# Batch 5's q by way of DRAM and DMA transposes, and every step in a new order

## The chip, the cores and the metric

The kernel runs on one core of one Trainium2 chip. A core has five engines that each take instructions in their own order: TensorE (PE in the profile; its weight loads stand apart as PEld), VectorE (DVE), ScalarE (ACT), GpSimd (POOL) and SyncE (SP). DMAs are issued by two of them: SP issues DMAs on a hardware queue, GpSimd on a software queue. The metric is the device time of one execution in microseconds.

## The reference

Two parts follow each other. Sliding-window causal attention over 8 batches of 8 heads, 576 positions and 64 channels; then a two-layer network on the result, laid out as 4608 tokens of 512 channels.

```python
scores = scale * np.matmul(q, k.transpose(0, 1, 3, 2))
rel = pos[:, None] - pos[None, :]
mask = (rel >= 0) & (rel < 64)
attn = softmax(np.where(mask, scores, -1e9))
x = np.matmul(attn, v).transpose(0, 2, 1, 3).reshape(4608, 512)
h = x @ w_in                       # 512 x 2048
g = h - np.tanh(h)
out = g @ w_out                    # 2048 x 512
```

(The softmax is written out in the reference; it is abbreviated here.) Inputs and output are float32; the kernel works in bfloat16 with float32 sums.

## The kernel before, in words

Heads are taken in pairs: pair g = 4b + r holds heads r and r + 4 of batch b, so there are 32 pairs. Tokens of x are taken in nine chunks of 512, and the 2048 hidden channels in sixteen parts m of 128. Each of these small pieces of work is a *step*, a Python function that issues its instructions; `STEPS` (line 557) gives every step a short name, and `PLAN` (line 581) is one long string of such names. `play` reads it from left to right, so **the order of the words is the order of the instructions on every engine and on every queue**; the scheduler is switched off (`tc.manual_schedule()`), and semaphores make a step wait for its inputs and for its buffers. A letter at the end of a name selects the engine: p GpSimd, a ScalarE, v VectorE, s SP. The steps that matter here:

- `lk`, `lq` (line 92) load k or q of a pair, `LQ.b` (line 114) loads q of a whole batch (576 KB), `lv`, `lt`, `LV.b.i` load v, `lr` (line 173) loads rows of k, `wi.0` to `wi.2` (line 189) load w_in in three parts and `wo.0` to `wo.3` w_out. All but the very first are issued on GpSimd's queue and cast to bfloat16 on the way.
- q reaches the layout of the scores in one of two ways. *By TensorE* (batches 0 to 5 before): `cq` (lines 88 or 90) rearranges the pair's rows into `qb`, `Ep.g` (line 261) makes six 96-row transposes into PSUM, and two evictions `Ea.g` and `Eb.g` (lines 88 or 90) write the halves of `qT`. *By DMA* (batches 6 and 7 before): `cz.g` (two copies on GpSimd, line 128) spreads the rows into `qz[g % 2]`, whose other columns are zero; `bo.g` (SP, line 133) writes that to DRAM, and `td.g` (SP, line 138) reads it back with a transposing DMA into `qT[g % 2]`. `z` (line 235) clears both `qz` once, on GpSimd; `mk` (line 220) clears pads of `kw`.
- k is transposed on TensorE (`Fp`, `Fc`) for batches 0 to 2, and by `tk.b.i` (SP, line 181), a transposing DMA from the loaded rows into `kw[b % 2]`, for batches 3 to 7.
- `Rp.g.i` are the scores of a third of a pair (three matmuls, line 300), `Rx` the exponentials (ScalarE, line 305), `M` the masking (VectorE, line 393). `Z.b` (VectorE, lines 166 and 167) copies v's rows across partition halves, in two copies, for the windows that straddle two blocks; `PP.g` (36 matmuls, line 418) multiplies two pairs by v and needs `Z`. `DR` and `DN` normalise.
- x is transposed on TensorE for batches 1 and 2 (`Xp`, `Xc`) and by SP's transposing DMAs (`Y.b`, line 472) from batch 3 on.
- `H.c.m` (four matmuls, line 487), `A.c.m` (tanh on ScalarE, line 495), `G.c.m` (subtraction on VectorE, line 501), `W.c.s.p` (four matmuls, line 526) and `O.c.s` (eviction and output DMA, line 542) are the network. `U.n` are n matmuls on zeros that fill TensorE's early waits.

`qT`, `qz`, `kw`, `vw` and the loaded rows of q and k exist twice, taken in turn, so a load waits until the last reader of two batches (or two pairs) earlier is done. In the steady part the words of attention for batch b + 2 or so stand among those of the network on earlier chunks.

The way by DMA in code:

```python
def cast_q(g):
    i = stage.pop((g, "q")).rearrange("p h (e d) -> p h e d", d=D)
    for h in range(2):
        nc.gpsimd.tensor_copy(qz[g % 2][:, h, :, 64 * h:64 * h + 64], i[:, h])

def bounce(g):
    t = dram.tile([2, S, 128], BF16, tag="q", name="qd")
    nc.sync.dma_start(out=t.rearrange("h (p e) c -> p h (e c)", e=E),
                      in_=qz[g % 2].rearrange("p h e c -> p h (e c)"))
    rows[g, "qd"] = t

def tr_dma(g):
    nc.sync.dma_start(out=qT[g % NR].rearrange("c h s -> c (h s)"),
                      in_=rows.pop((g, "qd")).rearrange("h s c -> (h s) c"), transpose=True)
```

Of the kernel before, what the change touches and what calls it, by code (L numbers as in the profile page):

```python
# [15 lines left out]
def kernel(  # L16
# [21 lines left out]
    M = d_ff // 128  # L38
# [515 lines left out]
    def subtract(c, m, s=None):  # L554
# [4 lines left out]
        z=lambda: [more_zeros(i) for i in range(2)],  # L559
# [16 lines left out]
    def play(script):  # L576
# [5 lines left out]
        mt.0 mv.0 mt.1 lk.3.p lq.0.s lk.1.p u ck.1.a lq.1.p LV.0.1 cq.0.a lk.0.s i mv.1 U.11 cq.1.v mq.1 U.1  # L582
        LV.0.3 Ep.1.3 Fp.1.2 Ec.1.3.v lq.3.p ck.0.v U.4 U.1.3 h Fc.1.2.a LV.0.2 Fp.0.2 LV.0.0 LV.0.4 Rp.1.1.4
        lk.2.p Ep.0.3 Ec.0.3.v lq.2.p Fc.0.2.a Rx.1.1.4 Rp.1.0.0 Rp.0.1.4 Rx.1.0.0 Fp.3.2 Ep.3.3 Rx.0.1.4
        Rp.0.0.0 Fc.3.2.v Z.0 Ec.3.3.a Rx.0.0.0 U.4 lk.5.p lk.7.p lq.5.p lk.6.p n Rp.3.1.4 P.0 Fp.2.2 D.0 Ep.2.3
        Rp.3.0.0 Fc.2.2.a lq.4.p lk.4.p Ec.2.3.v lq.7.p U.2 ck.5.v Rx.3.0.0 P.1 Rx.3.1.4 Fp.5.3 cq.5.v Rp.2.0.0
        Fc.5.3.a Rp.2.1.4 Rx.2.0.0 D.1 Rx.2.1.4 Ep.5.3 Xp.0.0.1.2 lv.1.1.1 P.3 wi.0 Eb.5.3.v wi.1 ck.4.v
        Ea.5.3.a wi.2 Xc.0.0.1.2.a Fp.4.3 Fc.4.3.a Rp.5.0.4 lv.1.1.0 lq.6.p D.3 lt.1 cq.4.v P.2 Rx.5.0.4
        lv.1.0.1 lv.1.0.0 Xp.0.0.0.3 Rp.5.1.4 D.2 Xc.0.0.0.3.a U.1.2 Xp.0.1.0.3 Xp.0.1.1.2 Rx.5.1.4 Xc.0.1.1.2.v
        U.1 mq.0 Rp.5.2.4 Xc.0.1.0.3.a H.0.1 A.0.1 H.0.0 ck.7.v Rx.5.2.4 G.0.1 H.0.2 wo.0 za.1.1.p lq.8.p A.0.0  # L590
        G.0.0 A.0.2 Ep.4.3 H.0.4 Eb.4.3.a wo.1 Ea.4.3.a A.0.4 ck.6.v G.0.2 H.0.3 Fp.7.3 Rp.4.2.4 lk.8.p H.0.5
        A.0.3 N Fc.7.3.v zb.1.0.p Rx.4.2.4 G.0.3 Fp.6.3 A.0.5 zb.1.1.p Rp.4.0.4 Rx.4.0.4 G.0.5 H.0.6 Rp.4.1.4
        G.0.4 A.0.6 Fc.6.3.a G.0.6 wo.2 wo.3 H.0.8 cq.6.v lq.9.p H.0.7 lk.9.p cq.7.v H.0.9 A.0.8 G.0.8 A.0.7
# [36 lines left out]
        G.3.2 tk.5.0 Ep.20.3 H.3.3 cq.22.a Rp.18.2.4 lr.6.1.1 lr.6.4.0 Rx.18.2.4 LV.5.2 H.3.4 lr.7.2.1 cq.23.v  # L630
# [75 lines left out]
```

## Time and profile before

| | |
|---|---|
| runs | 314.80, 314.82, 316.29 us; median 314.82 |
| the profiled execution | 316.02 us, its span 314.2 us |
| TensorE matmuls busy | 302.0 us, 96% of the span |
| VectorE, ScalarE, GpSimd busy | 188.3, 171.2, 111.4 us |
| first matmul of the network (H.0.1) | 25.58 us |
| last matmul ends | 310.7 us |
| DMA packets of the software queue | 69.1% of 16 engines' span |
| qd<-qz writes on SP | 8, 288 KB each, 3.4 us to landing |

The page gives busy time of each engine over the whole span; the windows cut it by stage, the list of waits tells for what an engine stood still, and the timeline shows single instructions in order of their start. A matmul record has the time from its start to its modelled end, so neighbouring matmuls overlap in the timeline; the time that a step takes from TensorE is the distance between the starts of neighbouring groups. A few matmul records are missing, so a gap of one matmul (0.216 us) inside a group of H or W is not a pause.

### The profile page before, as it was taken

The numbers are of one execution on the slowest core, as the hardware profiler recorded it, in microseconds if no ns is written. First come the engines' busy times: TensorE is split into PE (matmuls) and PEld (weight loads), VectorE is DVE, ScalarE is ACT, GpSimd is POOL, SyncE is SP. The second block draws the span as 40 slices with busy tenths as digits, with TensorE's granted clock in tenths as the row PEclk, the third lists the DMA queues.
The fourth block names the chain that finished last, engine by engine and source line by source line (L and its number), as shares of the span: only waits on it lengthen the run. The fifth ranks groups of instructions, "written<-read, shape, count | busy, mean of one in ns | idle before, by whom it ended". The sixth has DMA issues, their size and how long they took to land.

```text
span 314.2 us, 6083 instructions
## 1 busy us (share of the span) xinstructions
PE 302.0 (96%) x2385; PEld 165.1 (53%) x2413; DVE 188.3 (60%) x323; ACT 171.2 (55%) x320; POOL 111.4 (35%) x164
## 2 busy tenths in 40 slices
PE   6988999998999999999999999999999999999995
PEld 2565555655655556555555545555554444544444
DVE  1685987699857876667655545864674434343400
ACT  3677865488956867657355536444333543433311
POOL 8990655769909460492532540000000000000000
PEclk9999999999999999999999999999999999999999
DMA  9999999999999999997999996581004110010111
GB/s 156 149 169 206 170 203 147 184 102 153 131 147 119 143 184 165 132 133 160 166 167 193 195 202 154 111 179 40 34 35 109 57 45 33 33 37 33 67 69 67
DMA packets 113133, 39.11 MB, mean 124 GB/s; under 512 B 96336, under 2 KB 107600, under 8 KB 113104
## 3 DMA queue, kind: packets, MB, share of 16 engines
q0 software_dynamic: 72064, 18.06, 69.1%
q1 hardware_dynamic: 41040, 20.65, 28.9%
q8 instruction: 19, 0.31, 0.4%
q14 instruction: 10, 0.08, 0.1%
HBM read 36.70 MB, written 11.80 MB: 154 GB/s over the span
## 4 chain that ended last, share of the span: by engine, by line
PE 82%; POOL 6%; DMA 5%; DVE 4%; issue 1%; ACT 1%; POOLq 0%; DVEq 0%; ACTq 0%
PE ps L526 38%; PE ps L487 34%; DMA qall<-in_q_dram 5%; PE ps L300 4%; PE ps L418 3%; DVE gT L501 2%; POOL kall L108 1%; POOL vw L160 1%; PE ps L261 1%; POOL qall L108 1%; PE ps L519 1%; POOL wi L189 1%; PE ps L453 1%; DVE vw L167 1%; DVE qb L90 1%
## 5 line engine op out<-in xcount | busy, mean ns | idle before, releaser
L501 DVE TENSOR_TENSOR gT<-ps,th 128x512 bf16<-128x512 f32 x144 | 97.3, 688 | 80.6 <-ACT th L495 80.0
L487 PE MATMUL ps<-xT,wi 128*128 128x512 bf16 x576 | 141.6, 379 | 0.5 <-DMA wi<-in_moe_w_in_dram 0.3
L526 PE MATMUL ps<-w_out_sb,gT 128*128 128x512 bf16 x532 | 131.8, 379 | 1.4
L495 ACT ACTIVATE th<-ps 128x512 f32<-128x512 f32 x144 | 84.7, 597 | 78.3 <-PE ps L487 74.9
L487 PEld LDWEIGHTS <-wi 128*128 128x128 bf16 x576 | 62.0, 113 | 49.7 <-DMA wi<-in_moe_w_in_dram 0.5
L526 PEld LDWEIGHTS <-gT 128*128 128x128 bf16 x560 | 53.1, 98 | 56.9
L305 ACT ACTIVATE pt<-ps 128x384 bf16<-128x384 f32 (+2 forms) x92 | 45.8, 503 | 20.7 <-PE ps L300 19.5
L176 POOL DMA_DIRECT2D kall<-in_k_dram x50 | 37.1, 758 | 26.5 <-DMA kw<-kall 16.2
L160 POOL DMA_DIRECT2D vw<-in_v_dram x35 | 30.5, 877 | 11.2 <-PE ps L418 8.3
L88 ACT ACTIVATE ysb<-ps 128x512 f32<-128x512 f32 (+1 forms) x23 | 13.3, 578 | 28.4 <-PE ps L526 25.9
L393 DVE TENSOR_TENSOR pt<-pt,ps 128x1152 bf16<-128x1152 bf16 x28 | 20.7, 747 | 2.3 <-ACT pt L305 2.2
L300 PEld LDWEIGHTS <-kw 128*128 128x128 bf16 x180 | 14.4, 98 | 11.7 <-issue 0.4
L88 ACT ACTIVATE qt<-ps 64x576 bf16<-64x576 bf16 x30 | 19.3, 642 | 1.3 <-PE ps L300 0.3
L300 PE MATMUL ps<-qt,kw 128*128 128x128 bf16 x180 | 19.0, 219 | 0.0
L128 POOL COPY qz<-qall 96x384 bf16<-96x384 bf16 x16 | 7.6, 521 | 22.6 <-DMA qd<-qz 12.0
L438 DVE TENSOR_TENSOR xs<-ps,rcp 128x384 bf16<-128x384 f32 x28 | 15.0, 549 | 0.1
L418 PE MATMUL ps<-vw,pt 128*64 128x65 bf16 x504 | 10.7, 197 | 1.5 <-DVE vw L167 1.5
L418 PEld LDWEIGHTS <-pt 128*64 128x64 bf16 x504 | 9.3, 111 | 4.5 <-issue 2.8
L90 DVE COPY ysb<-ps 128x512 f32<-128x512 f32 x14 | 9.6, 686 | 2.6 <-PE ps L526 2.6
L225 PE MATMUL ps<-warm 128*128 128x512 bf16 x26 | 8.9, 478 | 2.2 <-DVE warm L206 2.1
L261 PE MATMUL ps<-ident,qb 96*128 96x96 bf16 x132 | 9.3, 206 | 1.4 <-DVE qb L90 1.4
L261 PEld LDWEIGHTS <-qb 96*128 96x128 bf16 x132 | 7.5, 97 | 4.5 <-DVE qb L90 1.9
(69 smaller groups left out, 169.6 us busy)
## 6 DMA issues: line engine op xcount, KB each, us to landing
out_dram<-ysb SPq DMA_DIRECT2D x35, 256.0 KB, 2.2
vw<-in_v_dram POOLq DMA_DIRECT2D x28, 128.0 KB, 6.0
qall<-in_q_dram POOLq DMA_DIRECT2D x5, 576.0 KB, 8.2
kall<-in_k_dram POOLq DMA_DIRECT2D x40, 64.0 KB, 5.6
qd<-qz SPq DMA_DIRECT2D x8, 288.0 KB, 3.4
w_out_sb<-in_moe_w_out_dram POOLq DMA_DIRECT2D x4, 512.0 KB, 9.2
kall<-in_k_dram POOLq DMA_DIRECT2D x11, 144.0 KB, 5.0
qall<-in_q_dram POOLq DMA_DIRECT2D x11, 144.0 KB, 5.0
```

Source lines behind the costliest of these rows:

```text
L88: nc.scalar.activation(o, i, ACT.Copy)
L160: nc.gpsimd.dma_start(out=w[:, 2 * i + 1, :, 0:D] if i < NF else w[64:128, 2 * i, :, 0:D], in_=v[b, :, 128 * i:128 * i + n].rearrange("h p ...
L176: nc.gpsimd.dma_start(out=token_rows(b)[0:c, i, :, h, :], in_=k[b, NP * h:NP * h + NP, 128 * i:128 * i + c].rearrange("r p d -> p r d"))
L261: nc.tensor.transpose(tp[:, e, :], src[:, e, :], ident[:P, :P])
L300: nc.tensor.matmul(sp[:, i], kt[:, 64 * j:64 * j + 128], qT[g % NR][:, :, 64 * j:64 * j + 64], start=first, stop=first or i == n - 1)
L305: nc.scalar.activation(PT[g % NPT][:, js[0]:js[0] + len(js), :].rearrange("p i (h t) -> p i h t", h=2), sp, ACT.Exp, scale=scale)
L393: nc.vector.tensor_tensor(p, p, mask.unsqueeze(1).to_broadcast([128, 2 * NJ, 64]), ALU.mult)
L418: nc.tensor.matmul(ps[r, bank, 65 * i:65 * i + 65], PT[(g + r2) % NPT][:, j, r], vw[b % 2][:, j, p0 + r2 + NP * h, :], start=True, stop=True)
L487: nc.tensor.matmul(hp, w_in_tile(ki, m), chunk_tile(c)[:, n.start // 64:n.stop // 64, ki % 2, 64 * (ki // 2):64 * (ki // 2) + 64], start=( ...
L495: nc.scalar.activation(th[:, n], hp, ACT.Tanh)
L501: nc.vector.tensor_tensor(gT[c][:, m, columns(s)], hp, th, ALU.subtract)
L526: nc.tensor.matmul(yp, gT[c][:, m, s * 128:(s + 1) * 128], w_out_sb[:, m, :], start=n == 1 and i == 0, stop=n == 4 and i == 3)
```

## The change

Batch 5's q (pairs 20 to 23) is taken out of the way by TensorE and put on the way by DMA: `cq.20` to `cq.23`, `Ep.20` to `Ep.23` and `Ea`, `Eb` of these pairs go; `cz.20` to `cz.23`, `bo.20` to `bo.23` and `td.20` to `td.23` come. No function is changed or added, and the number of all other steps is the same; but the whole `PLAN` is written in a new order, and about thirty evictions and casts (the letter at the end) go from ScalarE to VectorE or the other way. Among the moved steps: the order of the loads ahead of `wi.0`, `wi.1` and `wi.2`; `z`, which stood between `Ea.10` and `G.1.0` and now stands after `Eb.6`; `Y.3`, `tk.5` and `LQ.5` to `LQ.7`; and one `U.1.2`, which stood after `Ep.13`.

On SP's queue, the order from `O.1.2` to `O.2.2` was

```
O.1.2 Y.3 O.1.3 tk.5.4 tk.5.1 tk.5.2 O.2.0 tk.5.0 tk.5.3 O.2.1 bo.25 O.2.2
```

and is

```
O.1.2 Y.3 bo.20 O.1.3 tk.5.0 O.2.0 tk.5.1 tk.5.3 bo.21 td.20 bo.22 tk.5.2 tk.5.4 td.21 O.2.1 bo.23 O.2.2
```

Of the diff, the lines of PLAN that hold the steps spoken of:

```diff
--- before.py
+++ after.py
@@ -579,100 +579,100 @@
...
     PLAN = """
...
-        Fc.5.3.a Rp.2.1.4 Rx.2.0.0 D.1 Rx.2.1.4 Ep.5.3 Xp.0.0.1.2 lv.1.1.1 P.3 wi.0 Eb.5.3.v wi.1 ck.4.v
-        Ea.5.3.a wi.2 Xc.0.0.1.2.a Fp.4.3 Fc.4.3.a Rp.5.0.4 lv.1.1.0 lq.6.p D.3 lt.1 cq.4.v P.2 Rx.5.0.4
-        lv.1.0.1 lv.1.0.0 Xp.0.0.0.3 Rp.5.1.4 D.2 Xc.0.0.0.3.a U.1.2 Xp.0.1.0.3 Xp.0.1.1.2 Rx.5.1.4 Xc.0.1.1.2.v
...
-        G.0.4 A.0.6 Fc.6.3.a G.0.6 wo.2 wo.3 H.0.8 cq.6.v lq.9.p H.0.7 lk.9.p cq.7.v H.0.9 A.0.8 G.0.8 A.0.7
...
-        Rx.8.1.4 Rp.9.0.4 H.1.1 A.1.0 Eb.10.3.v A.1.1 H.1.2 cq.11.v Ea.10.3.v Fp.10.3 z G.1.0 Rx.9.0.4 G.1.1
...
-        Ea.11.3.a Eb.11.3.a G.1.5 mk H.1.7 lr.4.0.1 A.1.6 Rp.10.0.4 H.1.8 Ep.12.3 tk.3.2 LV.3.2 A.1.7 Z.2
...
-        U.1.2 Rp.11.2.4 lr.4.2.1 H.1.13 DN.8.2 Eb.13.3.a G.1.11 tk.3.1 Rx.11.2.4 DN.8.0 tk.3.0 H.1.14 LV.3.1
...
-        A.2.2 Eb.15.3.a G.2.2 Rp.14.1.4 LV.3.4 H.2.5 O.1.1.v Rx.14.1.4 Rp.14.0.4 Rx.14.0.4 H.2.4 A.2.5 Z.3
...
-        G.2.8 LV.4.3 G.2.9 lr.5.0.0 LQ.5 Rp.17.0.4 LV.4.2 Rx.17.0.4 PP.14 Eb.16.3.a DR.14 W.1.3.0 H.2.10
...
-        Rx.17.2.4 Rp.16.1.4 A.2.13 G.2.12 H.2.14 M.17 lr.5.3.1 Y.3 lr.5.1.1 cq.21.a A.2.14 LV.5.0 O.1.3.v
-        Rx.16.1.4 G.2.13 W.2.0.0 Ea.18.3.v tk.5.4 H.2.15 Eb.18.3.a cq.19.v A.2.15 tk.5.1 G.2.14 W.2.0.1 Ep.19.3
-        Rp.18.1.4 Rx.18.1.4 lr.5.3.0 LV.5.4 Ea.19.3.a Eb.19.3.a W.2.0.2 M.16 tk.5.2 H.3.0 G.2.15 A.3.0 cq.20.v
...
-        G.3.2 tk.5.0 Ep.20.3 H.3.3 cq.22.a Rp.18.2.4 lr.6.1.1 lr.6.4.0 Rx.18.2.4 LV.5.2 H.3.4 lr.7.2.1 cq.23.v
-        W.2.1.0 W.2.1.1 tk.5.3 DR.16 Ea.20.3.a M.18 LV.5.1 LQ.6 A.3.3 G.3.3 H.3.5 W.2.1.2 A.3.4 Eb.20.3.a
-        lr.6.2.1 Rp.19.2.4 lr.7.0.1 A.3.5 Ep.21.3 Rx.19.2.4 G.3.4 H.3.6 Rp.19.0.4 G.3.5 cz.25 DN.16.1 A.3.6
-        Rx.19.0.4 H.3.7 W.2.1.3 Rp.20.0.4 DN.16.0 lr.7.1.0 A.3.7 Rx.20.0.4 G.3.6 G.3.7 H.3.8 O.2.1.v Eb.21.3.a
-        Rp.20.2.4 A.3.8 DN.16.2 lr.6.3.0 H.3.9 lr.6.4.1 W.2.2.0 Rx.20.2.4 A.3.9 M.19 Ea.21.3.a PP.18 G.3.9 bo.25
-        G.3.8 Rp.21.1.4 H.3.11 Rx.21.1.4 Rp.20.1.4 H.3.10 Ep.22.3 DR.18 W.2.2.1 Eb.22.3.v W.2.2.2 A.3.10 LV.5.3
...
-        tk.6.2 Ea.22.3.a Rp.21.2.4 Ep.23.3 bo.24 A.3.13 M.20 G.3.10 H.3.12 G.3.13 W.2.3.1 W.2.3.2 DN.18.2 A.3.12
-        Rx.21.2.4 DN.18.0 G.3.12 Eb.23.3.a Ea.23.3.a Rp.22.1.4 H.3.14 cz.27 Y.4 Rx.22.1.4 H.3.15 Z.5 M.21 A.3.14
-        Rp.23.1.4 tk.6.4 G.3.14 bo.27 W.2.3.3 A.3.15 Rx.23.1.4 G.3.15 O.2.3.v PP.20 DR.20 H.4.1 cz.26 LV.6.4
...
-        lr.7.1.1 W.3.1.1 lr.7.3.0 LQ.7 LV.6.3 H.4.8 A.4.7 A.4.8 G.4.7 W.3.1.2 G.4.8 H.4.9 td.24 DR.22 A.4.9
...
-        A.5.2 G.5.2 H.5.4 W.4.0.3 A.5.3 td.27 G.5.3 M.25 tk.7.1 H.5.5 LV.7.0 Rp.27.1.4 cz.30 Rp.27.2.3 A.5.4
...
+        Rp.0.0.0 LV.0.4 Rx.0.0.0 ck.5.a lq.2.p mk Fc.3.2.v lk.2.p U.2 Z.0 Rp.3.1.4 P.0 U.1.3 Ep.2.3 lq.5.p
...
+        Rp.2.1.4 D.1 n lv.1.0.0 U.1.2 lv.1.0.1 Ep.5.3 Rp.2.0.0 Rx.2.1.4 lq.7.p lq.4.p Ea.5.3.v P.3 wi.0 U.1.2
+        D.3 Rx.2.0.0 lq.6.p Xp.0.0.1.2 cq.4.v wi.1 Eb.5.3.a Fp.4.3 Fc.4.3.a P.2 Xp.0.0.0.3 Xc.0.0.0.3.a D.2
+        lk.7.p Rp.5.0.4 N Xc.0.0.1.2.v Rx.5.0.4 Xp.0.1.0.3 Xc.0.1.0.3.v Xp.0.1.1.2 Rp.5.1.4 wi.2 Ep.4.3
...
+        H.0.6 A.0.6 Rp.4.1.4 H.0.7 wo.1 Fc.6.3.a lq.9.p G.0.5 za.1.1.p zb.1.1.p A.0.7 wo.2 H.0.8 Ep.7.3 A.0.8
...
+        Rp.7.0.4 PP.4 cq.8.v Eb.6.3.a z H.0.14 lk.10.p lq.11.p lq.10.p G.0.12 H.0.13 lk.11.p zb.1.3.p A.0.14
...
+        A.1.7 Z.2 G.1.6 Rx.11.1.4 PP.8 tk.3.2 Rp.11.0.4 G.1.7 H.1.9 lr.5.4.1 A.1.8 H.1.10 G.1.8 Rx.11.0.4
...
+        Rp.12.0.4 Xp.2.1.0.3 lr.4.4.0 Rx.12.0.4 G.1.14 W.1.0.3 Xc.2.1.0.3.v Rp.13.2.4 Ep.14.3 O.1.0.a H.2.1 LQ.5
+        Eb.14.3.v Rx.13.2.4 A.2.1 G.2.1 Rp.13.1.4 H.2.0 W.1.1.0 LV.3.4 Ea.14.3.a W.1.1.1 lr.4.4.1 Rx.13.1.4
...
+        H.2.5 Z.3 O.1.1.v PP.12 tk.4.0 A.2.5 Rx.14.0.4 cz.21 G.2.2 tk.4.4 H.2.4 DR.12 lr.5.2.1 Rp.15.2.4
...
+        H.2.6 cz.20 Rx.14.2.4 Ea.17.3.a H.2.9 M.15 A.2.6 Rp.17.1.4 lr.5.0.0 A.2.9 Ep.16.3 M.14 O.1.2.a G.2.6
...
+        G.2.10 H.2.12 G.2.11 A.2.12 lr.6.4.0 H.2.13 Y.3 cq.19.v G.2.12 W.1.3.3 Rx.16.2.4 lr.5.1.1 A.2.13
+        Rp.17.2.4 bo.20 Ep.18.3 H.2.14 Rx.17.2.4 O.1.3.a Rp.16.1.4 A.2.14 G.2.13 lr.5.2.0 Ea.18.3.a Rx.16.1.4
+        M.17 LV.4.2 lr.5.3.1 lr.5.1.0 G.2.14 H.2.15 A.2.15 M.16 lr.5.3.0 G.2.15 W.2.0.0 H.3.0 W.2.0.1 H.3.1
+        Eb.18.3.v tk.5.0 Rp.18.1.4 A.3.0 A.3.1 Ep.19.3 G.3.0 Rx.18.1.4 lr.5.4.0 W.2.0.2 Rp.18.0.4 H.3.2
...
+        H.3.3 LV.5.0 tk.5.1 tk.5.3 PP.16 Rp.18.2.4 W.2.1.0 bo.21 td.20 cz.22 Rx.18.2.4 M.18 Rp.19.2.4 bo.22
+        A.3.3 Rx.19.2.4 H.3.4 A.3.4 Rp.19.0.4 G.3.3 W.2.1.1 H.3.5 W.2.1.2 DR.16 G.3.4 lr.7.3.0 tk.5.2 tk.5.4
+        DN.16.1 H.3.6 W.2.1.3 A.3.5 G.3.5 H.3.7 DN.16.0 Rx.19.0.4 A.3.6 DN.16.2 lr.6.4.1 td.21 cz.23 O.2.1.a
+        Rp.20.0.4 cz.24 A.3.7 G.3.6 M.19 lr.6.3.1 H.3.8 G.3.7 W.2.2.0 PP.18 W.2.2.1 DR.18 Rx.20.0.4 A.3.8 G.3.8
...
+        Rp.20.1.4 G.3.9 Rx.20.1.4 lr.6.0.1 bo.23 H.3.11 Rp.21.0.4 Rx.21.0.4 O.2.2.v H.3.10 Rp.21.2.4 DN.18.2
+        A.3.11 A.3.10 M.20 LV.5.2 G.3.11 td.22 Rx.21.2.4 W.2.3.0 cz.25 W.2.3.1 DN.18.0 H.3.13 G.3.10 td.23
...
+        lr.6.2.0 Rx.25.0.3 tk.6.2 H.4.8 bo.27 LV.6.0 td.24 A.4.8 G.4.7 Rp.25.1.4 LV.7.1 H.4.9 O.3.1.v LQ.7
...
+        Rp.25.2.3 H.4.15 bo.28 bo.29 td.27 H.4.14 A.4.15 W.3.3.3 G.4.15 Rx.25.2.3 A.4.14 G.4.14 H.5.1 cz.30
+        O.3.3.a H.5.0 A.5.1 A.5.0 lr.7.0.0 Rx.24.2.4 G.5.0 W.4.0.0 W.4.0.1 H.5.2 G.5.1 W.4.0.2 A.5.2 LV.6.4 Z.6
...
     play(PLAN)
...
```

## The prediction

> **What bounds the kernel now.** I read the busy shares first, then the chain that ended last, then busy time by stage. From the page:
>
> ```profile
> PE 302.0 (96%) x2385; PEld 165.1 (53%) x2413; DVE 188.3 (60%) x323; ACT 171.2 (55%) x320; POOL 111.4 (35%) x164
> ...
> PEclk9999999999999999999999999999999999999999
> ...
> PE 82%; POOL 6%; DMA 5%; DVE 4%; issue 1%; ACT 1%; POOLq 0%; DVEq 0%; ACTq 0%
> ```
>
> TensorE is busy 96% of the span at its full clock, and most of the last chain is TensorE; POOL and DMA in the chain are the loads of the first 25 us. The windows by stage (columns: stretch, length, then busy us of PE, PEld, DVE, ACT, POOL):
>
> ```profile
> 25.50:71.10 45.60, 45.21 (x389) 26.35 (x393) 36.54 (x70) 31.43 (x60) 26.44 (x37) 1.00 1.33 168
> 71.10:72.90 1.80, 0.28 (x10) 0.23 (x9) 1.77 (x2) 1.80 (x5) 1.80 (x2) 1.00 1.17 274
> 72.90:210.00 137.10, 136.27 (x1139) 76.05 (x1155) 94.57 (x159) 84.97 (x167) 61.24 (x88) 1.00 1.43 155
> 210.00:314.00 104.00, 100.22 (x546) 50.85 (x554) 40.97 (x64) 38.35 (x68) 0.00 (x0) 1.00 0.17 54
> ```
>
> The reader sees one real hole: 1.80 us at 71 with 0.28 us of TensorE work. From 73 to 210 only 0.83 of 137.10 us is idle, so there a TensorE instruction taken away shortens the span by its own time, and a late input lengthens it. (The last 3.5 us are the last eviction and output; these steps are not changed in kind.) The waits of TensorE name the hole and the only input wait on a weight:
>
> ```profile
> PE ps L418 <- DVE vw L167: 1.5, 1, 1.5
> ...
> PE ps L487 <- DMA wi<-in_moe_w_in_dram: 0.3, 1, 0.3
> ```
>
> and the timeline shows what was under the hole:
>
> ```profile
> 68.99 3.24 POOL L235 MEMSET qz<- 96x1536 bf16 x2
> ...
> 69.53 1.38 DVE L166 COPY vw<-vw 64x2080 bf16<-64x2080 bf16 x1
> ...
> 70.92 1.86 DVE L167 COPY vw<-vw 64x2080 bf16<-64x2080 bf16 x1
> ...
> 72.83 0.76 PE L418 MATMUL ps<-vw,pt 128*64 128x65 bf16 x36 [1.52 <-DVE vw L167]
> ```
>
> The two copies of batch 2's v rows (Z.2), which PP.8 needs, took 1.38 and 1.86 us while GpSimd cleared qz; the medians of these lines over seven batches are 0.697 and 0.695. Together they lost 3.24 - 1.39 = 1.85 us.
>
> **The change, part by part.** The profiled execution took 316.02 us, 1.82 more than its span of 314.2, and stands 1.20 above the median of the runs (314.82). I sum the changes on its span and carry them to the median.
>
> 1. TensorE work taken away. Ep.20 to Ep.23 are 4 x 6 = 24 transposes (L261). In TensorE's timeline Ep.21's six start at 129.51 and the next matmul at 129.76, Ep.20's at 123.72 and 123.99: 0.25 to 0.27 us for six, with 0.255 taken. 4 x 0.255 = 1.02 us, all in the dense stage: -1.02. One warm-up matmul (U.1.2 at 77 us, as wide as those of H, which take 0.86 us for four) leaves the dense stage for the wait ahead of the weights: -0.22.
>
> 2. Evictions and casts taken away. Eight evictions of q (7 on ScalarE at 642 ns, one on VectorE at 750) and four casts (two of 834 ns, two of 393) are 4.5 + 0.75 + 1.67 + 0.79 = 7.7 us. ScalarE and VectorE are 62% and 69% busy in the dense stage and TensorE waits there for neither, so 0; some thirty other evictions change between the two engines, and both stay below 70%: 0 as well. If that cover went, a wait like those of 0.2 to 0.5 us in the list of waits would appear.
>
> 3. The clearing of qz (two memsets) moves ahead, to about 40 us, before the loads of batch 2's v. Z.2 then has its 1.39 us and PP.8's wait goes, but for a remainder of 0.1: -1.42. Next late at that place would be the masks (0.75 us on VectorE), ready before. Beside the memsets there lies at 40 us other VectorE work, subtractions of 0.69 us, which the chain tanh to W needs only much later.
>
> 4. The loads ahead of the weights are ordered anew on GpSimd's queue. Before, w_in's first part was issued at 17.50 and landed at 25.54, the third landed at 33.19, and H.0.8, which needs it, began at 33.30. Now two v loads and two small memsets (0.34 us each) come ahead of the first part and two go behind, which puts its issue at about 18.65; lq.6 comes between the first and second parts, lk.7 between the second and third. That queue is never empty from 4 to 50 us. The first part lands between 25.2 (the same bytes are ahead of it) and 26.7 (issue + 8.0, the shortest landing of w_in). The third has some 290 KB more ahead of it, 1.7 us at the 168 GB/s of this stage's window, less what goes behind it: about 34 to 35.8. One more step of H (0.86 us) is placed ahead of H.0.8, so that of the 0.8 to 2.6 us a part is filled. Bounds: 0 (as before) and +2.5; I take +1.0, the middle of the two landings less the H moved ahead.
>
> 5. Batch 5's q goes the long way. Eight GpSimd copies (L128, median 508 ns, so 1.02 us for a pair), four DMAs out on SP's queue (0.53 us each to issue, 3.4 to land) and four transposes (1.31 to issue, 3.1 / 3.7 / 5.3 to land):
>
> ```profile
> L138 SPq DMA_TRANSPOSE qt<-qd x8: 1227/1314/1837, 156.5 to 206.2; - x8
> DMA to landing us min/median/max: 3.1/3.7/5.3
> ```
>
> SP issues in order, so what is behind a transpose is late by its wait. td.20 stands behind O.2.0, two transposes of k (tk.5.1, tk.5.3) and bo.21: O.2.0 was issued at 123.06 before, and 0.34 + 2 x 1.22 + 0.53 after it makes td.20 at about 127. It lands at 130.1 to 132.3; Rp.20.0.4, its first user, was at 132.31 and comes about 1 earlier: margin +1.2 to -1.0. tk.5.4, behind td.20, bo.22 and tk.5.2, has 3 to 6 us to land and a margin of 0 to 1; td.21 about 1.2. Also pushed along this queue: Y.3, which x of batch 3 needs for H.3.0, had 1.85 us between landing and use and now has about 0.8. Before, transposes on this queue took up to 9.1 us at 98 us, when loads ran beside them. Bounds: 0 (all land at the minimum) and +3.3 (three steps each 1.1 late); I take +0.4.
>
> 6. GpSimd's own queue. The copies cz.20 to 23 stand among the loads of k and v: a copy that waits for its q (LQ.5) or for the DMA that empties its buffer (12.0 us in two waits before, in lines L128) holds every load behind it. LV.3.4 stands behind LQ.5, LV.6.4 behind cz.30, each with 0 to 3 us by the landings of before (median 6.0 for a load of v): take +0.1, with ends 0 and 1.5.
>
> At item 3 a rule speaks against the change. By the Trainium skill, "SBUF — State Buffer", "Who interferes with whom", VectorE and GpSimd share a port as an exclusive lock, so a fast VectorE copy and a GpSimd operation shut each other out; the rows of Z.2 (1.38 and 1.86 against 0.70) agree. By that rule each new GpSimd copy could do to a VectorE copy what the memsets did. The rows for it are in the second rival.
>
> Sum: -1.02 - 0.22 - 1.42 + 1.0 + 0.4 + 0.1 = -1.16: 314.9 for an execution like the profiled one, 313.66 against the median, say **313.6**. A measurement of this kernel can tell about 0.5% (1.57 us; the three runs alone lie 1.5 apart), so below 313.25 is faster and above 316.39 slower.
>
> **The rivals.**
>
> *All of the gain stays.* TensorE has scores and transposes of batch 1 to do while w_in is late, and the transposes land near their minimum of 3.1. For it: before, the wait for w_in was only 0.3 us, and transposes between 190 and 207 us took 3.1 to 3.4. Against: H.0.8 began 0.1 us after its weights landed, so it had no slack. Then -2.66 + (0 to 0.5): 312.2 to 312.7.
>
> *The blocked copy returns elsewhere.* cz.21 (two GpSimd copies, 1.02 us) is placed right after Z.3, which ran at 95.76 to 97.33, just ahead of PP.12; if they meet, Z.3 stretches by 1.0 (the copies' time) to 1.85 (as Z.2 did) and PP.12 waits. For it: item 3's rows. Against: four pairs of such copies between 134 and 151 left no wait of TensorE over 0.3 us, and cz.21 must wait for a load of 576 KB. Then 313.66 + 1.0 to 1.85: 314.7 to 315.5.
>
> *Slower: batch 5's transposes land late.* One mechanism, on SP between 120 and 140 us: batch 5's k transposes, batch 5's q and the output share the queue and the DMA engines with the loads of k for batches 6 and 7. If the landing is 8 us, as tk.5.4 and Y.3 had at 112 to 116 (8.3 and 8.7), instead of 3.7, td.20 lands at 135 and Rp.20.0.4, at about 131.4, waits 3.7 us, with td.21 and tk.5.4 behind it for another 1. The sum turns positive from a total lateness of 1.6 us, and passes the 0.5% above 3.1. For it: those two rows. Against: from 122 us on, before, all on this queue landed within 2.0 to 3.7 us until 142. Then 313.66 - 0.4 + 3.7 (to 4.7): 317.0 to 318.0; at a landing of 6 us, 315.0.
>
> **How the numbers follow.** Forecast as summed 0.38 (313.0 to 314.5: a quarter of it under the bound of faster); all of the gain 0.26; the returned block 0.16; late transposes 0.20, of which a quarter ends inside 0.5%. Faster: 0.26 + 0.10 = 0.36. Slower: 0.15, with 0.04 from the returned block and a late w_in together (+2.5 instead of 1.0): 0.19. The rest, 0.45, is the same. The range leaves out the end of the first rival and the worst half of the last: 312.2 to 316.8; the forecast's own range is 313.0 to 314.5.
>
> **What would show it.** PP.8 without a wait and Z.2's lines at 0.7 each (item 3); the group L261 with 108 instead of 132 matmuls and the dense stage 1.2 us shorter between the same steps (1); the landing of w_in and the start of H.0.8 at 34 to 35.8 (4); landings of the transposes L138 against the starts of Rp.20 to Rp.23, and a wait of TensorE for qt or kw near 131 (5); Z.3's lines at 0.7 or above 1 (second rival). The prediction is wrong if TensorE has a wait of over 1 us that these do not name, for then the new order has opened a place that I did not look at.

## The result, and the profile after

The changed kernel took 318.99 to 320.66 us, median 320.09; the kernel before, beside it, had a median of 315.56. The ratio is 1.0136, 95% interval [1.0088, 1.0184]: 4.3 us slower, outside the predicted range (312.2 to 316.8) and on the other side of no change. A second measurement gave 1.0119 [1.0076, 1.0163]. Every ratio here compares fast runs alone: an execution over 1.5% above the fastest of its kernel is left out. The profiled execution took 320.26 us, its span 318.6, 4.4 more than before.

From the page of the changed kernel: the busy shares, the SP queue's row (its share was 28.9% before, of a span of 314.2) and the chain that ended last:

```profile
PE 302.2 (95%) x2361; PEld 164.1 (52%) x2389; DVE 187.9 (59%) x324; ACT 165.4 (52%) x307; POOL 116.0 (36%) x172
...
q1 hardware_dynamic: 46608, 23.01, 34.9%
...
PE 56%; DMA 26%; POOL 10%; issue 3%; SPq 2%; DVE 1%; ACT 1%; POOLq 0%; ACTq 0%
```

TensorE carried 82% of the last chain before and carries 56% now; DMA went from 5 to 26%. The windows by stage (columns as before):

```profile
25.50:71.10 45.60, 43.04 (x376) 24.79 (x377) 32.08 (x62) 34.29 (x64) 27.91 (x38) 1.00 1.50 164
71.10:72.90 1.80, 1.80 (x12) 1.01 (x11) 1.75 (x3) 1.77 (x4) 1.11 (x2) 1.00 1.47 275
72.90:210.00 137.10, 132.41 (x1095) 72.78 (x1109) 91.49 (x155) 76.64 (x150) 64.10 (x92) 1.00 1.54 169
210.00:318.00 108.00, 104.56 (x575) 53.24 (x583) 48.17 (x75) 39.25 (x71) 0.00 (x0) 1.00 0.21 61
```

The hole at 71 us is gone. The dense stage, where TensorE was idle for 0.83 us, has 4.69 us of idle time, and the first stage 2.56 where it had 0.39. TensorE's waits name what it stood still for (of the list, those behind the start of the network):

```profile
PE ps L300 <- DMA kw<-kall: 2.4, 2, 1.9
PE ps L487 <- DVE gT L501: 1.5, 3, 0.9
PE ps L487 <- DMA wi<-in_moe_w_in_dram: 1.1, 2, 0.9
...
PE ps L487 <- DMA xT<-xs: 0.8, 1, 0.8
...
PE ps L418 <- DMA vw<-in_v_dram: 0.4, 1, 0.4
```

Four of the five are late DMAs. Of the fifth, the longest part (0.9 us, at H.1.3) is one in disguise: `G` stood behind cq.13 on VectorE, which waited 1.51 us for batch 3's q. The largest, in the timeline:

```profile
102.39 4.48 SPq L181 DMA_TRANSPOSE kw<-kall  x2
...
105.41 0.23 PE L300 MATMUL ps<-qt,kw 128*128 128x128 bf16 x1 [0.48 <-DMA kw<-kall]
...
107.55 0.28 PE L300 MATMUL ps<-qt,kw 128*128 128x128 bf16 x2 [1.91 <-DMA kw<-kall]
```

Rp.17.1.4 waits in its middle for tk.4.2, batch 4's k, which was issued at 99.03 and took 8.47 us to land, before the first of the eight added DMAs was issued (bo.20, at 116.77).

To see the whole, I added up the time between the starts of neighbouring matmuls beyond what each shape takes (gaps of one missing record left out), in us:

| | before | after | after, second profile |
|---|---|---|---|
| start of H.0.1 | 25.58 | 26.29 | 27.69 |
| waits, from there to 50 us | 0.80 | 1.76 | 0.52 |
| 50 to 100 | 1.68 | 1.09 | 0.80 |
| 100 to 115 | 0.00 | 2.75 | 0.03 |
| 115 to 160 | 0.08 | 1.27 | 1.43 |
| 160 to 210 | 0.06 | 0.93 | 2.50 |
| sum | 28.20 | 34.09 | 32.97 |

5.9 us more of waiting stand against spans that differ by 4.4 us; the 1.5 between them are what is left for the work saved. (The list of waits counts whole idle time only and gives up to 0.4 us less for one wait.)

### The profile page after: what moved, and what is told of

Read it like the earlier page. It is cut to its first block, busy times and chain, and to the rows that moved or that the text cites. A ratio compares the mean times of both kernels' runs of the same rounds, so it can differ in the third digit from the quotient of the medians.

```text
span 318.6 us, 6043 instructions
## 1 busy us (share of the span) xinstructions
PE 302.2 (95%) x2361; PEld 164.1 (52%) x2389; DVE 187.9 (59%) x324; ACT 165.4 (52%) x307; POOL 116.0 (36%) x172
## 4 chain that ended last, share of the span: by engine, by line
PE 56%; DMA 26%; POOL 10%; issue 3%; SPq 2%; DVE 1%; ACT 1%; POOLq 0%; ACTq 0%
PE ps L526 27%; PE ps L487 24%; DMA vw<-in_v_dram 9%; DMA kall<-in_k_dram 5%; DMA kw<-kall 4%; DMA qall<-in_q_dram 3%; POOL vw L160 3%; DMA wi<-in_moe_w_in_dram 2%; PE ps L300 2%; PE ps L418 2%; DMA xT<-xs 2%; POOL kall L108 1%; SPq L472 1%; POOL kall L176 1%; POOL qall L108 1%
## 5 line engine op out<-in xcount | busy, mean ns | idle before, releaser
L305 ACT ACTIVATE pt<-ps 128x384 bf16<-128x384 f32 (+1 forms) x92 | 45.4, 503 | 24.3 <-PE ps L300 23.0
L300 PE MATMUL ps<-qt,kw 128*128 128x128 bf16 x180 | 20.2, 219 | 2.4 <-DMA kw<-kall 2.4
L128 POOL COPY qz<-qall 96x384 bf16<-96x384 bf16 x24 | 12.4, 553 | 27.3 <-DMA qd<-qz 20.4
L88 ACT ACTIVATE ysb<-ps 128x512 f32<-128x512 f32 (+1 forms) x20 | 11.5, 575 | 18.4 <-PE ps L526 11.3
L90 DVE COPY ysb<-ps 128x512 f32<-128x512 f32 x17 | 11.7, 687 | 15.1 <-PE ps L526 15.0
L88 ACT ACTIVATE qt<-ps 64x576 bf16<-64x576 bf16 x25 | 16.0, 640 | 3.2 <-PE ps L261 2.3
L88 ACT ACTIVATE kt<-ps 128x576 bf16<-128x576 bf16 x8 | 5.2, 651 | 8.2 <-PE ps L261 8.1
L108 POOL DMA_DIRECT2D qall<-in_q_dram x11 | 7.2, 653 | 6.2 <-DVE pt L393 5.5
```

The costliest lines, as they stand in the source:

```text
L88: nc.scalar.activation(o, i, ACT.Copy)
L300: nc.tensor.matmul(sp[:, i], kt[:, 64 * j:64 * j + 128], qT[g % NR][:, :, 64 * j:64 * j + 64], start=first, stop=first or i == n - 1)
L305: nc.scalar.activation(PT[g % NPT][:, js[0]:js[0] + len(js), :].rearrange("p i (h t) -> p i h t", h=2), sp, ACT.Exp, scale=scale)
```

## The experiments

Two theories went into the first runs. *Order*: each wait is the fault of one step's place and goes when the step is moved. *Route*, later sharpened to *DMA*: the DMAs of batch 5's q, by the room they take, make other DMAs late, and a mended wait comes back elsewhere. Ratios are to the kernel before, timed beside each run; its medians were 315.4 to 316.1 us.

**1. The memsets of qz, alone** (kernel before, one word moved).

```diff
-lv.1.3.1 lr.3.3.0 lk.10.p ... lr.3.0.1 z lr.3.0.0      (GpSimd's order)
+lv.1.3.1 z lr.3.3.0 lk.10.p ... lr.3.0.1 lr.3.0.0
```

> The kernel before with z (the two memsets of qz on GpSimd) moved ahead, behind lv.1.3.1, to about 45 us; nothing else. If the two copies of Z.2 were long only because of the memsets beside them, they take 0.7 us each, the wait of 1.5 us at PP.8 goes, and the time is 1.3 to 1.5 us less (ratio about 0.9955). If the memsets do the same harm to the casts and evictions beside them at 45 us, or PP.8 waits for something else by then, less than 0.5 us is won.

Ratio 1.0001 [0.9982, 1.0020]: nothing. Yet the mechanism is there: the copies of Z.2 fell to at most 0.82 and 0.79 us and the wait at PP.8 is gone. Another has come, 38 us later:

```profile
110.20 0.23 PE L300 MATMUL ps<-qt,kw 128*128 128x128 bf16 x1 [1.07 <-DMA kw<-kall]
```

TensorE reached Rp.16.2 1.3 us earlier than before (108.86 instead of 110.14), but the transpose that it needs (tk.4.4) landed 2.2 us later (110.15 instead of 107.98); its rows had come behind lr.6.2.0 and LV.3.4, which were later too. With tk.4.4 where it was, there would have been no wait. Why the loads were later is not shown, and this is one execution.

**2. The same, with a load that held that transpose moved.**

```diff
-LV.3.4 lr.6.2.0 lr.4.3.0 lr.5.0.1      (GpSimd's order; z moved as in 1)
+LV.3.4 lr.4.3.0 lr.6.2.0 lr.5.0.1
```

> The kernel before with z moved ahead (as in the run on z alone) and lr.4.3.0 moved ahead of lr.6.2.0 on GpSimd's queue; lr.6.2.0 waits there for a transpose to empty its rows, and held lr.4.3.0, and with it tk.4.3 and tk.4.4, until 100 us. Theory 'order': the wait of 1.1 us for kw at Rp.16.2, in which the gain of z came back, goes too, and the time is 1.2 to 1.4 us under before (ratio 0.996). Theory 'DMA' (until about 205 us the 16 DMA engines have as much to do as TensorE, so an earlier TensorE waits for the next late DMA, wherever it is): a wait of about 1 us shows at another kw, qt or xT, and the ratio is 0.999 to 1.001.

Ratio 0.9968 [0.9946, 0.9989], faster than before by 0.1 to 0.5%. With the warm-up matmul moved as well:

```diff
-Ep.13.3 U.1.2 Rp.11.2.4                (in addition)
+Ep.13.3 Rp.11.2.4                      (U.1.2 beside the first U.1.2)
```

> The kernel before with z moved ahead and lr.4.3.0 ahead of lr.6.2.0 (ratio 0.9968 in that run), and with the warm-up matmul U.1.2 that stands behind Ep.13 moved to the wait ahead of w_in. Theory 'order': 0.2 us less than without the last move, ratio 0.995 to 0.997. Theory 'DMA': a wait for a DMA between 100 and 115 us takes the 1.4 us back, as in the run on z alone, ratio 0.999 to 1.001.

Ratio 0.9984 [0.9959, 1.0009], which the first value lies inside; the last move is not to be seen. The second interval holds 1 as well, so of the 1.42 us that the wait was worth these two runs show about 0.5 to 1.0, and only the first clear of noise. In the windows of the second kernel TensorE has no idle time from 85 to 205 us:

```profile
85.00:115.00 30.00, 30.00 (x260) 16.81 (x258) 21.30 (x36) 20.14 (x39) 17.55 (x23) 1.00 1.71 143
115.00:160.00 45.00, 45.00 (x371) 24.63 (x368) 31.12 (x54) 29.65 (x57) 17.46 (x26) 1.00 1.20 162
160.00:205.00 45.00, 45.00 (x345) 24.18 (x344) 27.11 (x45) 22.27 (x44) 13.22 (x20) 1.00 1.13 163
```

Its span is 313.4 us, 0.8 less than before, with H.0.1 1.1 us later (26.65). (The first kernel's profile is of its longest execution, 320.45 us, and is not read here.)

**3. Single waits of the changed kernel mended.** First LQ.5, behind which the last rows of batch 4's k were loaded:

```diff
-LQ.4 lr.4.3.0 lr.4.4.0 LQ.5 LV.3.4 lr.4.4.1 lr.4.2.1 lr.4.0.0 lr.4.1.0 lr.4.2.0 lr.4.3.1 cz.21 ... cz.20
+LQ.4 lr.4.3.0 lr.4.4.0 LV.3.4 lr.4.4.1 lr.4.2.1 lr.4.0.0 lr.4.1.0 lr.4.2.0 lr.4.3.1 LQ.5 ... cz.21 cz.20
```

> The changed kernel, but LQ.5 (batch 5's q, 576 KB) stands behind the six last loads of batch 4's k rows instead of ahead of them, and cz.21 stands directly ahead of cz.20. Theory 'order' (the loss is made of single waits that the new order of the loads and DMAs makes; the wait of 2.1 + 0.6 us at Rp.17.1.4 comes from tk.4.1 and tk.4.2, which wait for rows behind LQ.5): the wait of TensorE for kw falls from 2.4 us to under 0.5, and the time by 2 to 2.7 us, to about 317.5 (ratio to before about 1.006). Theory 'route' (the twelve DMAs and eight GpSimd copies more make all loads and transposes land late, so that a mended wait comes back elsewhere): the wait comes back at Rp.20 or Rp.21, where td.20 and td.21 land late, and the time stays at 319.5 to 320.5.

319.25 us, ratio 1.0134 [1.0079, 1.0189]. The wait at Rp.17.1.4 went (0.03 us between 100 and 115), but 4.0 us of waits stand between 115 and 210, where there were 2.2:

```profile
PE ps L487 <- DMA xT<-xs: 2.3, 2, 1.6
...
PE ps L418 <- DMA vw<-in_v_dram: 0.7, 1, 0.7
```

Then three others at once, in the changed kernel itself:

```diff
-H.1.1 ... cq.13.v Rx.9.0.4 ... G.1.2   |  td.23 tk.6.4 bo.24 Y.4  |  cz.28 cz.29 cz.30 lr.7.0.0 LV.6.4
+H.1.1 ... Rx.9.0.4 ... G.1.2 cq.13.v   |  td.23 Y.4 tk.6.4 bo.24  |  LV.6.4 cz.28 cz.29 cz.30 lr.7.0.0
```

> The changed kernel with three words moved: cq.13.v behind G.1.2 (VectorE waited in it 1.5 us for LQ.3, with G.1.0 and G.1.1 behind it, and TensorE 0.9 to 1.1 us at H.1.4), Y.4 ahead of tk.6.4 and bo.24 (0.96 us at H.4.1), LV.6.4 ahead of cz.28 (0.53 us inside PP.24). Theory 'order': these three waits go, 2.3 to 2.5 us less, about 317.7 (ratio about 1.007), with the wait at Rp.17.1.4 as it was. Theory 'route': later waits take their place, 319 to 320.5.

Slower: 325.97 us, ratio 1.0311 [1.026, 1.0362]. The three waits went, w_in was waited for longer (3.2 us instead of 1.1), and two larger waits came at 169 and 177 us:

```profile
169.01 0.39 PE L300 MATMUL ps<-qt,kw 128*128 128x128 bf16 x2 [2.33 <-DMA kw<-kall]
177.27 0.34 PE L300 MATMUL ps<-qt,kw 128*128 128x128 bf16 x3 [3.04 <-DMA qt<-qd]
```

td.24 took 10.06 us to land there, where it took 5.80 in the changed kernel. *Order* fails in both runs. *Route* had looked for the first at Rp.20 and Rp.21, and the waits came elsewhere.

**4. The route, in the order of before.** cq, Ep, Ea, Eb of pairs 20 to 23 are taken out and these put in:

```diff
+lr.5.1.1 cz.20 | LV.5.0 cz.21 bo.20 bo.21 | LV.5.2 cz.22 cz.23 | tk.5.3 td.20 bo.22 bo.23
+Rp.19.0.4 td.21 | Rp.20.1.4 td.22 | Rp.21.2.4 td.23      (tk.6.2 and bo.24 moved behind Y.4)
```

> The kernel before in its own order, with batch 5's q alone put on the way by DMA: cq, Ep, Ea, Eb of pairs 20 to 23 go, and cz, bo, td of these pairs are put where their inputs and buffers are free (cz.20 and cz.21 among the loads at 111 to 112 us, td.20 behind tk.5.3, td.21 to td.23 behind the scores that free their buffer; tk.6.2 and bo.24 behind Y.4). Theory 'order': the 24 transposes are saved and no load is late, 0.7 to 1.0 us less than before (ratio 0.997 to 0.998). Theory 'route': waits for qt, for xT or for v of 1 to 4 us come up between 120 and 160 us, ratio 1.002 to 1.01.

332.77 us, ratio 1.0554 [1.0511, 1.0597]: worse than either theory said. One wait makes more than half of it:

```profile
144.33 0.50 PE L300 MATMUL ps<-qt,kw 128*128 128x128 bf16 x3 [9.87 <-DMA qt<-qd]
```

td.21 and LQ.6, side by side from 129 to 144 us, took 15.1 us each. So LQ.6 was put ahead, where it lands first:

```diff
-lr.6.4.0 LV.5.2 cz.22 cz.23 lr.7.2.1 LV.5.1 LQ.6
+lr.6.4.0 LQ.6 LV.5.2 cz.22 cz.23 lr.7.2.1 LV.5.1
```

> The kernel before with batch 5's q on the way by DMA as in the run on the route alone (332.8 us), but LQ.6 ahead of LV.5.2 on GpSimd's queue, so that it lands before td.20 to td.22 are issued. Theory 'DMA', first part: transposes and a load of a whole batch's q that run side by side slow each other, td.21 and LQ.6 both took 15.1 us there, and the wait of 9.9 us for qt at Rp.21.1.4 came from it; apart they take 3.5 to 5 and 7 to 10 us, the wait falls below 1 us, and the time falls by 8 to 12 us, to 321 to 325. Theory 'order' (a single place on SP's or GpSimd's queue was wrong): the wait of 9.9 us stays, 331 to 333.

The four executions lie between 326.85 (the profiled one) and 333.26 us, ratio 1.0402 [1.0332, 1.0472], between the two expectations. The 9.9 us fell to 3.9 (td.21 took 9.2 us beside loads of k and v), not below 1: LQ.6 was a part of it only. These two runs also bear on my places: td.21 has 5.4 us between the scores that free its buffer and those that need it, too few for a transpose that takes 9.2 or 15.1. They do not say what the best place would cost.

**5. The DMAs alone.** Eight idle DMAs in the kernel before, whose results nobody reads, while batch 5's q stays on TensorE (xb: a write of 288 KB to DRAM; xt: its transposing read into a spare tile):

```diff
+LV.5.0 xb.20 xb.21 | tk.5.3 xt.20 xb.22 xb.23 xt.21 | bo.25 xt.22 | O.2.2.a xt.23
```

> The kernel before, whole and in its own order, with eight DMAs more on SP's queue that nobody waits for: four writes of qz (288 KB each) to DRAM tiles of their own and four transposing reads of these into a tile of their own, at the places where batch 5's q would go that way (115 to 145 us). Theory 'DMA' (the eight DMAs of the route cost time by what they take from the DMA engines and from SP's queue, not by their own lateness): waits for kw, qt, xT or v come up behind 115 us where there were 0.14 us before, 1.5 to 3 us in sum, ratio 1.005 to 1.010. Theory 'lateness' (only the scores that wait for a late td lose): no new wait over 0.3 us, ratio 0.999 to 1.002.

323.94 us, ratio 1.0238 [1.0191, 1.0285]. But in this form the writes read qz, and cz.25 waited 10.4 us for them with loads of v behind it; that is a queue, not the engines. The second form takes this wait away:

```diff
+xb reads a spare tile instead of qz      (cleared behind LV.3.4)
-bo.25 xt.22 | O.2.2.a xt.23
+O.2.1.v xt.22 | bo.25 xt.23
```

> The kernel before with the same eight idle DMAs, but so that no step of the kernel stands behind them: the writes read a tile of their own (cleared on GpSimd at about 87 us, where it has nothing to do), so that cz does not wait for them, and all eight are issued where SP was idle before (115, 126 to 134, 134 and 136 to 142 us). Theory 'queue' (in the first run with idle DMAs the loss of 7.5 us came from cz.25, which waited 10.4 us for the writes out of qz and held loads of v, and from Y.4 behind an idle transpose): both waits go, no new one over 0.3 us, ratio 0.998 to 1.003. Theory 'DMA' (the engines that carry the DMAs are full): loads and transposes of the kernel still land later, 1 to 4 us of waits behind 115 us, ratio 1.004 to 1.012.

322.16 us, ratio 1.0203 [1.0153, 1.0252]: 5 to 8 us, more than either theory said, for DMAs whose results no step reads. The stage from 115 to 160 us, first of the kernel before, then of this one:

```profile
115.00:160.00 45.00, 44.68 (x365) 24.68 (x370) 31.19 (x54) 30.41 (x58) 18.94 (x29) 1.00 1.38 153
```

```profile
115.00:160.00 45.00, 41.25 (x340) 22.42 (x338) 28.07 (x49) 26.45 (x51) 17.44 (x26) 0.96 1.41 185
```

TensorE is idle 3.4 us more there while the DMA engines move 185 GB/s instead of 153; and its granted clock is 0.96 instead of 1.00, about 1.8 us of the 45 by an estimate (0.04 x 45). The waits come in two ways. One is in the load of batch 6's q, first before, then with the idle DMAs (KB, us to landing):

```profile
qall<-in_q_dram POOLq DMA_DIRECT2D x1, 576.0 KB, 7.0
```

```profile
qall<-in_q_dram POOLq DMA_DIRECT2D x1, 576.0 KB, 10.8
```

cz.25, on GpSimd, waits for that load until 139.02 instead of 134.06, and the loads of v behind it are as much later; Z.5 waits for them, and PP.20 for Z.5 (1.4 us). The other is SP's queue. All four xt write the same spare tile, so each waits until the one before has landed, and SP issues nothing meanwhile:

```profile
SPq L150 <- DMA scr<-dq: 10.6, 3, 6.4
```

xt.22 was issued at 140.68, when xt.21 had landed, and xt.23 at 145.54, when xt.22 had. O.2.2 behind them went out at 147.15 instead of 141.99 and Y.4 at 149.73 instead of 145.03; Y.4 took 3.7 us to land, as before (3.6), but H.4.1 waited 1.9 us for it. So the run shows both that DMAs of two queues slow each other and that a transpose which waits holds its queue; its 5 to 8 us are not the price of a fuller set of DMA engines alone.

**6. The same eight DMAs taken out of the new order.** On the kernel of the first run of 3:

```diff
-bo.20 bo.21 bo.22 bo.23 td.20 td.21 td.22 td.23      (the scores of batch 5 use what stands in qT)
```

> The changed kernel with LQ.5 behind the loads of batch 4's k rows (319.25 us in that run), and bo.20 to bo.23 and td.20 to td.23 left out: the four writes and four transposing reads of batch 5's q. The scores of batch 5 then use what stands in qT; TensorE, GpSimd and all other DMAs do the same work in the same order. Theory 'DMA': the waits at H.4.1 (1.8 us), at H.5.1 (0.8) and inside PP.24 (0.9) come from DMA engines that had these eight DMAs to carry as well; they go, and the time is 315.0 to 316.5. Theory 'order': only what stood directly behind them on SP's queue gains, under 1 us; 318.3 to 319.3.

317.86 us, ratio 1.0053 [1.0028, 1.0079], against 1.0134 [1.0079, 1.0189]: about 2.5 us, with intervals that just meet. From 115 to 160 us TensorE is never idle:

```profile
115.00:160.00 45.00, 45.00 (x354) 24.19 (x353) 30.23 (x50) 25.21 (x49) 20.49 (x32) 1.00 1.22 142
```

The waits at H.4.1 and H.5.1 went, the one inside PP.24 (0.7 us) stayed: LV.6.4 stands behind cz.30 whatever batch 5 does. So the first two hang on the eight DMAs, the third on *order*, and the sum lies between the two expectations. By which way the eight DMAs cost their time is left open here too. Without them Y.4 landed in 3.4 instead of 5.5 us, but SP also issued it at 142.31 instead of 145.21, and either would cover the 1.6 us of H.4.1; and on GpSimd cz.22 and cz.24 no longer waited (4.3 and 2.1 us) for bo.20 and bo.22 to empty qz.

**7. The new order, with batch 5's q back on TensorE.**

```diff
-cz.20 ... cz.23, bo.20 ... bo.23, td.20 ... td.23
+G.2.15 cq.20.v | Rx.18.2.4 Ep.20.3 | Rx.19.2.4 Ea.20.3.a Eb.20.3.v | M.18 cq.21.v | Rp.19.0.4 Ep.21.3 | Rx.19.0.4 Ea.21.3.a Eb.21.3.a
+M.19 cq.22.v | Rp.20.1.4 Ep.22.3 | Rx.20.1.4 Ea.22.3.a Eb.22.3.v | DN.18.1 cq.23.v | Rp.21.2.4 Ep.23.3 | Rx.21.2.4 Ea.23.3.a Eb.23.3.a
```

> The changed kernel with LQ.5 behind the loads of batch 4's k rows (319.25 us), and batch 5's q put back on TensorE: cz, bo, td of pairs 20 to 23 go, cq, Ep, Ea, Eb of these pairs come back between the scores of batches 4 and 5. What stays is the new order. Theory 'DMA': TensorE has 1.0 us more to do, but the waits of 3.5 us behind 148 us go: 316.5 to 317.5, so the route costs more than it saves. Theory 'order': the waits stay, 320 to 320.5.

322.0 us, ratio 1.0208 [1.0158, 1.0259]: both theories missed, since it is no faster than with the route (1.0079 to 1.0189; the intervals overlap). The waits behind 148 us shrank from 3.5 to 1.1 in the list of waits, but the evictions made a new one: 0.9 us at Ep.21, for Eb.20 on VectorE, which had itself waited 0.8 for Ea.20 on the busy ScalarE. I chose these places by hand, and the run shows no more than this: in these places, the new order without the route gains nothing over before.

**8. The loads ahead of w_in.** On the kernel of the first run of 3:

```diff
-n lv.1.0.0 lv.1.0.1 lq.7.p lq.4.p wi.0 lq.6.p wi.1 lk.7.p wi.2 lt.1 ... zb.1.0.p wo.0 wo.1 lq.9.p za.1.1.p
+n lq.7.p lq.4.p wi.0 lq.6.p wi.1 lk.7.p wi.2 lv.1.0.0 lv.1.0.1 lt.1 ... wo.0 wo.1 lq.9.p zb.1.0.p za.1.1.p
```

> The changed kernel with LQ.5 behind the loads of batch 4's k rows (319.25 us), and lv.1.0.0 and lv.1.0.1 (128 KB each) behind wi.2 instead of ahead of wi.0, with zb.1.0, which reads them, beside za.1.1. Theory 'order': w_in's parts land 1.2 to 1.5 us earlier (25.0 and 34.5 us), H.0.1 and H.0.8 start as much earlier, and the time falls by 1.0 to 1.4 us, ratio 1.008 to 1.010. Theory 'DMA': the stage is earlier, but the waits behind 100 us grow by the same, ratio 1.012 to 1.014.

326.88 us, ratio 1.0346 [1.0313, 1.038]. w_in's parts landed at 24.71 and 34.00 us, 1.5 and 2.0 earlier than in the changed kernel, as expected. But za.1.0 on VectorE reads these v rows, and I had left it at its place:

```profile
35.37 0.31 DVE L90 COPY vw<-vw 64x520 bf16<-64x520 bf16 x1 [8.61 <-DMA vw<-in_v_dram]
```

All subtractions stood behind it, and TensorE waited 8.1 us. The time says nothing on w_in; what an earlier w_in is worth was not measured.

**9. The changed kernel again.**

> The changed kernel once more, unaltered, for a second profile and a narrower interval. Theory 'places' (an order fixes where TensorE waits): the waits are where they were, 2.7 us for kw at Rp.17.1.4, about 1 at H.1.4 and at H.4.1, 0.5 inside PP.24, and the time is 319 to 320.7. Theory 'crowd' (how long a transpose takes beside the loads varies from one execution to the next): the sum of the waits behind 50 us is again 4 to 8 us, but at least two of these four places show under 0.3 us and others take their part.

319.76 us, ratio 1.0119 [1.0076, 1.0163]. TensorE's waits in this second profile:

```profile
PE ps L487 <- DMA wi<-in_moe_w_in_dram: 2.1, 1, 2.1
PE ps L487 <- DMA xT<-xs: 1.6, 2, 1.0
PE ps L418 <- DMA vw<-in_v_dram: 1.4, 1, 1.4
```

Rp.17.1.4, 2.75 us in the first, waits 0.03 here: tk.4.2 landed in 6.04 us instead of 8.47. The wait at H.1.3 (the expectation calls it H.1.4) fell from 1.06 to 0.34, just above the 0.3 that *crowd* had named, or to 0.2 in the list of waits, while w_in, H.4.1 and PP.24 cost more. So two of the four places cost in both profiles and two come and go, and the sum of the table falls by 1.1 only (the clock was 0.993 over this execution, which fits a span that is no shorter). Two profiles favour *crowd*, on a base of a few fixed places; they do not prove it.

## Why the prediction was wrong

- **Step 5 failed.** It priced batch 5's DMAs by SP's order and by the lateness of each (+0.4, at most +3.3). Against the scores that use them their landings came as forecast, though all was some 4 us later by then: td.20 landed at 134.45 (forecast 130.1 to 132.3), 0.55 us ahead of the weights of Rp.20.0.4, and td.21 to td.23 with 0.1 to 1.1 us to spare; no score of batch 5 waited over 0.3 us. What was left out is what they do to all others, on the 16 DMA engines and in the two queues that wait for them. They add 5568 packets and 2.36 MB to SP's queue; its share times the span is 90.8 us of the 16 engines before and 111.2 after (a sum of packet times; a packet of a transpose took 18 ns in the median at 184 us, with little beside it, and 31 ns at 98 to 100 us, beside loads, before the change). Idle DMAs of this kind cost 6.4 us in the old order, part of it by SP's queue, and leaving them out of the new one gained about 2.5. The page of before had the line for it, the DMA row with 9 tenths in every slice but one up to 188 us:

```profile
DMA  9999999999999999997999996581004110010111
```

The prediction read TensorE's 96% as the only full resource. Nine tenths here say that a packet was in flight, not that no more bytes fit: with the idle DMAs the stage from 115 us moved 185 GB/s instead of 153, and the load of experiment 5 took 10.8 us instead of 7.0.

- **The margins were the other half.** Step 5 took a transpose of q to land in 3.1 to 5.3 us, as those of 156 to 206 us had before. Beside loads, transposes took 4 to 10 us (td.24 4.6 to 10.1, tk.5.0 9.5), and the new order has margins of 1 us and less at twelve transposes where the one before had it at one. The largest single wait (tk.4.2, 2.75 us) was in batch 4's k, not in batch 5's q: LQ.5, which cz.20 and cz.21 need, stands ahead of its rows in the new order. The prediction followed LQ.5 only to LV.3.4.
- **Step 3 was right at its place and wrong in the sum.** The wait at PP.8 went, as forecast; but its "next late" was sought among VectorE's masks. Experiment 1 found a wait 38 us on, at a transpose, and no gain in the time; with a load moved as well, about half of the 1.42 us came out (experiment 2). Another new wait, of VectorE in cq.13 for batch 3's q (0.9 us at H.1.3), was not forecast at all.
- **Step 4 was right in mechanism, and its size was too small, within its bounds.** Forecast +1.0 with a bound of 2.5; measured 0.71 in the start of H.0.1 and 0.96 in the waits up to 50 us, 1.7 together, and 1.8 in the second profile. w_in landed at 26.24 (25.2 to 26.7 forecast) and 36.03 (34 to 35.8). One pair of profiles is rough for this: H.0.1 began between 25.24 and 27.54 us in the eight profiles with the first stage of before, and between 26.14 and 27.69 in the six with the new one.
- **Step 6** named the two places: LV.3.4 had no wait, LV.6.4 cost 0.4 and 1.4 us in the two profiles, against 0.1 taken and 1.5 as the end.
- **Steps 1 and 2 were right.** L261 has 108 matmuls, the table above leaves 1.5 us for the work saved (1.24 forecast), and no wait of the network for the moved evictions came up. By the last letters of the words, 55 evictions and casts change engine, 19 of them of the output, not some thirty.
- **The rivals.** The blocked copy at Z.3 did not happen: no copy of Z took over 1.06 us and PP.12 did not wait for one. So the rule of the Trainium skill that was weighed at step 3 ("SBUF — State Buffer", "Who interferes with whom"), the exclusive port of VectorE and GpSimd, agrees with Z.2's rows (0.82 and 0.79 us at most without the memsets, experiment 1) but did not decide. The slower rival had the right kind, transposes that land late, with the wrong ones and the wrong place: it looked between 120 and 140 us only.
- A page of the Trainium skill bears on step 5: "DMA: Bandwidth & Descriptors", "Issuing engines are not separate DMA queues", says that DMAs of all issuing engines run on the same 16 DMA engines and interleave. By that rule loads on GpSimd's queue become later when SP's queue gets more, and the trace agrees: 7.0 against 10.8 us for LQ.6 in experiment 5.

What stays open: how the 4.3 us divide. About 2.5 are the eight DMAs in the new order (experiment 6), 1.7 the first stage (table); that leaves the gains to be eaten by the waits between, which differ from one execution to the next. Open too is how the price of the eight DMAs divides between the DMA engines and the queues that stand still for them; idle transposes into four tiles of their own would tell.

## What to carry to other kernels

An engine at 96% does not rule out a second busy resource: look at the DMA row, and when it stands at 9 in the stage of the change, charge new DMAs for what they do to every DMA in flight and to every step behind them in their queue. A wait that is removed makes everything behind it earlier, so ask which transfer that was just in time will be late by the same amount. Test a DMA's price with idle copies that nobody reads, and make sure that none of the kernel's own steps reads or writes the tiles they use, and that the idle DMAs do not wait for each other.

## What the runs showed that I had not expected

- **Transposes and loads slow each other.** Counted by their starts in each whole microsecond from 85 to 210 us in the DMA records of fourteen profiles (all but that of the first run of experiment 2), where transposes ran in the microseconds around it too, SP's transposes moved 670 packets of 256 B in the median when nothing else ran (half of the values between 423 and 907), 311 beside loads of k and v rows (packets of 128 B; 184 to 436), and 126 beside loads of q (packets of 768 B; 74 to 209). By the medians the 1152 packets of one td are an estimated 1.7 us of transfer alone, 3.7 beside k and v, and 9.1 beside q. "Advanced Engine Details and Errata" of the Trainium skill, "X-Bar Transpose (TRN2)", expects 350 to 400 GB/s of a transpose; the most that one microsecond held here is 1121 packets, 287 GB/s (two transposes in flight, nothing else), and the median alone is 172 GB/s. The measurement decides.
- **Long waits go with a lower clock.** In the first run of experiment 4 the granted clock falls to 0.8 and 0.5 in the slices from 132 to 148 us, around and behind the wait of 9.9 us, and to 0.977 over the execution; TensorE thus loses more than the wait. It is the same in experiment 5 (0.7 from 152 to 160 us, behind waits up to 153.5) and 8 (0.6 from 32 to 41 us, around the wait of 8.1). That the wait is its cause was not tested, and the second kernel of experiment 2 has 0.8 in the slice from 24 to 31 us, with no wait over 0.4 us from 22 to 32 us in the list.
